# Two mixer layers on one core: normalised rows one step later in the first inverse stage, and another order for the last three rows before the second transform

## The chip, the core and the metric

The kernel runs on one core of a Trainium2 chip. Five engines work side by side, each through its own list in order: TensorE (PE in the profile, with its weight loads as PEld), VectorE (DVE), ScalarE (ACT), GpSimd (POOL) and SyncE (SP, which issues most of the transfers here). They wait for each other through semaphores. The metric is the time of one execution on the device, in microseconds (us); lower is better.

## The reference

Two kinds of layer alternate over an activation `x` of 2048 tokens by 640 channels, each kind twice and with the same weights both times:

```python
# A: global filter in the frequency domain
X = rfft2(x, axes=(-2, -1)) * (w_r + 1j * w_i)
y = irfft2(X, s=(S, D), axes=(-2, -1))

# B: token mixer, on the token axis, shared over channels
h = layernorm(x)                                   # over the channels
u = gelu(einsum("bsd,sf->bdf", h, w1) + b1)
y = einsum("bdf,fs->bds", u, w2) + b2              # then transposed back

x = x + A(layernorm(x)); x = x + B(layernorm(x))
x = x + A(layernorm(x)); x = x + B(layernorm(x))
```

S is 2048, D is 640, F is 1728, all in float32.

## The kernel before

The 2048 tokens lie as 16 rows of 128 partitions by 640 values (`NJ` = 16); one row of tokens is the unit of most loops. Products of 16-bit halves stand in for float32 ones: a value is kept as a high part and a low part (`fh`, `fl`; `hh`, `hl`; `wh`, `wl`), and three products (high by high, high by low, low by high) are summed in PSUM. A high part is written by ScalarE, the low part by VectorE as the difference. PSUM holds four tiles of two banks each (`big`), taken in turn.

`run` executes, twice: `a1` (transform along the tokens and channels, filter, first inverse), `a2` (last two inverse products, which give the new rows, and the layernorm in front of the mixer), and `b1st` or `b2nd` (the mixer). The first layer A's forward product `s1` is done at the start; the second one's is done inside `b1st`, row by row, as its rows become ready.

**`a2`, the inverse stage.** Its loop has one step a row, `i`, and works on several rows at a time. In step `i` TensorE makes `id_mm(i)`, 16 products, and `is1_mm(i-1)`, 6 products, whose operands are `eh` (ScalarE, from the result of `id_mm`) and `el` (VectorE, from the same result less `eh`). ScalarE copies part of the result of `is1_mm(i-2)` to `ec`, VectorE and then GpSimd add the result into the row `xt`, VectorE takes the row's statistics (`st`, `mv`, `v`, in the step after), GpSimd makes `r` and `nb` from them (one step later still), and ScalarE writes the normalised row `hf`, for rows 0 to 7 also its high part `hha`. Rows are loaded by SyncE into five buffers (`xload`), so a load waits until ScalarE has normalised the row five places earlier. `self.pin` holds the instructions of these loops in the order of the code. Behind the loop, `b1st` starts with the weights of the first two tiles of `w1`. Tile 13 of `w1` is the doubled one: 64 columns stand in it twice, and `wsplit` writes its high and low parts in halves, first ScalarE (`hi`), then VectorE (`lo`), one call for each of two chunks of eight rows of weights. Next `hl`, the low parts of the 16 normalised rows, is made on VectorE, and TensorE multiplies with them.

**The last rows of `b1st`.** Its second loop runs over the 16 rows of tokens, `j`. For each, TensorE sums the product with `w2` (82 products) into PSUM; ScalarE had added the bias to the old row, VectorE adds the product (`xt`), SyncE stores the row, and the row is prepared for the second layer A: statistics and `r`, `nb`, the normalised row `z` (`a0_norm`, ScalarE), sums and differences `eo` (`a0_fold1`, GpSimd) and `f` (`a0_fold2`, VectorE), `fh` (ScalarE), `fl` (VectorE). Then `s1` of the row: 15 small products on TensorE, `s1h` (ScalarE), `s1l` (VectorE). `pend` lists rows that are prepared and whose `s1` is still to come, and `flush(k)` issues them until `k` are left. The weights of the next row are split (`wsplit`) during the present row's product. Row 15 differs: its product is made for one half of the channels and then for the other, and `a0_tail` prepares it without waiting for the normalisation. In the kernel before, row 14's second half of the preparation stands in the middle of row 15's product, and its `fl` and `s1` stand inside `a0_tail`.

What follows, `a1`, starts with `dstage(0)`, whose products read `s1h` and `s1l` of all 16 rows.

All of these instructions go through the class `Pin`, so that the trace shows them under line 59; they are told apart by the names of the tiles.

Of the kernel before, what the change touches and what calls it, by code (L numbers as in the profile page):

```python
# [66 lines left out]
class Layers:  # L67
# [308 lines left out]
    def a0_tail(self, j, z, st, pend):  # L376

        V, G, T, p = self.V, self.G, self.T, self.pT
        mv = self.stats2(p, st)
        v = self.t(p, [128, 1], F32, "v", 2)  # L380
        V.tensor_scalar(v, mv[:, 1:2], self.CA, self.CB, op0=ALU.mult, op1=ALU.add)
        m2 = self.t(p, [128, 1], F32, "nm", 2)
        V.tensor_scalar(m2, mv[:, 0:1], 2.0, None, op0=ALU.mult)
        eo = self.t(p, [128, 646], F32, "eo", 2)
        v2 = lambda a, o, w: a[:, o:o + 2 * w].rearrange("p (a b) -> p a b", a=2)[:, :, 0:160]
        za, zb = v2(z, 1, 161), v2(z, 321, 160)
        G.tensor_tensor(v2(eo, 322, 161), za, zb, op=ALU.subtract)
        r = self.t(p, [128, 1], F32, "r", 2)
        G.tensor_tensor(r, v, self.mh, op=ALU.pow)
        V.scalar_tensor_tensor(v2(eo, 1, 161), za, m2, zb, op0=ALU.subtract, op1=ALU.add)  # L390
        V.tensor_scalar(eo[:, 0:162:161], z[:, 0:162:161], mv[:, 0:1], None, op0=ALU.subtract)
        sc = S1S / (ZS * TS)
        m = self.tM[j // 4]
        eb = eo[:, 0:644].rearrange("p (a b) -> p a b", a=2)
        ea, eb = eb[:, :, 0:160], eb[:, :, 161:321]
        fs = []
        for i, (c, w) in enumerate(((slice(0, 128), 512), (slice(128, 160), 128))):
            f = self.t(p, [128, w], F32, f"ft{i}", 1)
            f4 = f.rearrange("p (c b) -> p c b", c=4)
            V.tensor_tensor(f4[:, 0::3], ea[:, :, c], eb[:, :, c], op=ALU.add)  # L400
            V.tensor_tensor(f4[:, 1:3], ea[:, :, c], eb[:, :, c], op=ALU.subtract)
            if i:
                V.tensor_copy(f[:, 95:128:32], eo[:, 160:482:321])
            fh, fl = (self.t(p, [128, w], F16, f"{a}t{i}", 1) for a in ("fh", "fl"))
            T.activation(fh, f, AF.Identity, scale=r)
            fs.append((f, fh, fl))
        ps = []
        for k, f, fh in pend:
            ps.append((k, self.a0_s1(k, *self.a0_lo(f, fh))))
            self.a0_s1h(*ps[-1])  # L410
        qs = []
# [300 lines left out]
    def a2(self, li):  # L712
# [68 lines left out]
        for i in range(NJ + 5):  # L781
            has = [0 <= i - k < NJ for k in range(6)]
            if has[0]:
                pd[i] = id_mm(i)
            if has[1]:
                k = i - 1
                eh, ps = eo[k], pd.pop(k)
                el = elow(ps, eh)
                if not first and i == NJ:
                    self.pss0 = self.big()  # L790
                    for j in HA:
                        for a in range(2):
                            mm(self.pss0[:, a, :320], self.w[0][0][:, j], self.hh[j][:, a], start=j == 0, stop=False)
                p1[k] = is1_mm(eo.pop(k), el, tIM[k // 4][:, k % 4])
            if first and i == 10:
                next(sc)
            if has[4]:
                v, mean = vs.pop(i - 4)
                r = self.t(p, [128, 1], F32, "r", 2)
                G.tensor_tensor(r, v, self.mh, op=ALU.pow)  # L800
                b = self.t(p, [128, 1], F32, "nb", 2)
                G.tensor_scalar(b, mean, r, -1.0, op0=ALU.mult, op1=ALU.mult)
                rb[i - 4] = r, b
            if has[2]:
                k = i - 2
                x, ps = xt[k], p1.pop(k)
                o = ps[:, 1]
                e = self.t(p, [128, 324], F32, "ec", 2)
                T.activation(e[:, :322], ps[:, 0, :322], AF.Copy)
                V.tensor_tensor(v2(x, 160, NL), v2(x, 160, NL), v2(o, 161, 1), op=ALU.subtract)  # L810
                V.tensor_tensor(x[:, :NL], x[:, :NL], o[:, :NL], op=ALU.add)
                if first and i == 11:
                    next(sc)
                G.tensor_tensor(v2(x, 160, NL), v2(x, 160, NL), v2(e, 161, 1), op=ALU.add)
                G.tensor_tensor(x[:, :NL], x[:, :NL], e[:, :NL], op=ALU.add)
            if has[4]:
                r, b = rb.pop(i - 4)
                f = self.hf[i - 4]
                T.activation(f, xt.pop(i - 4)[:, :D].rearrange("p (a b) -> p a b", a=2), AF.Identity, scale=r, bias=b)
                if i - 4 in HA:  # L820
                    T.activation(self.hh[i - 4], f, AF.Copy)
            if 1 <= i and i + 1 < NJ:
                xt[i + 1] = xload(i + 1)
            if has[2]:
                nc.sync.dma_start(self.xs[li + 1][i - 2], xt[i - 2][:, :D])
            if has[3]:
                st = self.stats1(p, xt[i - 3])
                m = self.stats2(p, st)
                v = self.t(p, [128, 1], F32, "v", 2)
                V.tensor_scalar(v, m[:, 1:2], (1.0 + EPS) / ZS ** 2, EPS * EPS / ZS ** 2, op0=ALU.mult, op1=ALU.add)  # L830
                vs[i - 3] = v, m[:, 0:1]
            if has[0]:
                eo[i] = ehigh(pd[i])
            if i == 3:
                self.wload(1)
                self.wopen(1)
            if first:
                if i in (6, 7):
                    self.scan1(1, (i - 6,))
                if i == 8:  # L840
                    sc = self.scale1(1, at=lambda: p1[i - 1][:, 1, 400:401])
                    next(sc)
            if i in (12, 13):
                self.wsplit(1, (i - 12,), lo=False)
            if i in (1, 4, 8):
                mload()
        self.pin = False
# [81 lines left out]
    def b1st(self, li):  # L929
# [7 lines left out]
                T.activation(self.hh[j], self.hf[j], AF.Copy)  # L937
        sc = {m: self.scale1(m) for m in range(2, NFT + NJ)}
        self.pin = True
        self.wsplit(1, hi=False)  # L940
        self.wload(2)
        self.scan1(2)
        self.h = []
# [168 lines left out]
        def flush(k):  # L1112
            while len(pend) > k:
                self.s1_all(*pend.pop(0))

        for j in range(NJ):
            wh, wl = self.w.pop(NFT + j)
            ahead(NFT + j, (wh, wl))
# [3 lines left out]
            if j + 2 < NJ:  # L1122
                xts.append(load(j + 2))
            xt = xts[j][:, :D]
            T.activation(xt, xt, AF.Identity, bias=self.b2[:, j:j + 1])
            x2 = xt.rearrange("p (a b) -> p a b", a=2)
            tail = j == NJ - 1
            ps = self.big()
# [2 lines left out]
            if tail:  # L1131

                order.sort(key=lambda q: q[1])
                st = self.t(p, [128, 2, 6], F32, "st", 2)
                self.pin = True

            def half(a):
                V.scalar_tensor_tensor(x2[:, a], pss[a][:, :320], c2, x2[:, a], op0=ALU.mult, op1=ALU.add)
# [2 lines left out]
            for i, (ft, a) in enumerate(order):  # L1141
                if tail and i == NFT:
                    half(0)
                    flush(0)
                    pend.append((j - 1, *self.a0_hi(self.a0_fold2(late))))
                if i in (4, 8):
                    next(steps, None)
                if i in (6, 7):
# [11 lines left out]
            if tail:  # L1160
                half(1)
                nc.sync.dma_start(self.xs[li + 1][j], xt)
                self.a0_tail(j, xts[j], st, pend)
                self.pin = False
                break
            V.scalar_tensor_tensor(x2, ps[:, :, :320], c2, x2, op0=ALU.mult, op1=ALU.add)
            nc.sync.dma_start(self.xs[li + 1][j], xt)
            flush(1)
            r, b = self.stats_r(p, *self.stats(p, xt, self.CA, self.CB))
            late = self.a0_fold1(self.a0_norm(xt, r, b))  # L1170
            if j < NJ - 2:
                pend.append((j, *self.a0_lo(*self.a0_hi(self.a0_fold2(late)))))
        self.pop("a0")
        self.pop("u")
        self.pop("wr3")
# [798 lines left out]
```

## Time and profile before

| | |
|---|---|
| median of 3 runs | 1012.19 us (1011.85, 1012.19, 1015.22) |
| profiled execution | 1010.95 us |
| its span, first to last instruction | 1009.1 us |
| mean granted TensorE clock | 0.981 |
| VectorE busy | 781.1 us (77%) |
| ScalarE busy | 577.0 us (57%) |
| GpSimd busy | 297.9 us (30%) |
| first `a2` | 130 to 188 us |
| first `b1st`, from its first product to row 15's last | 183 to 556 us |
| second `a1` starts | 564.7 us |

TensorE is busy in most of the span, so a gain comes from stretches in which it stands still, or from fewer products. A row of the timeline gives the start in the span, the duration, the engine, the operation with what it writes and reads, and the partitions by elements. In brackets behind it stands the idle time of the engine ahead of it, with the operation that ended last before it went on. A row marked x4 stands for four instructions in a row, its duration for all of them together.

### The profile page before, as it was taken

How to read it: one execution, taken by the hardware profiler on the slowest of the kernel's cores; microseconds unless marked ns; L12 is line 12 of the kernel's file. 1: busy time of each engine (PE TensorE's matmuls, PEld its weight loads, DVE VectorE, ACT ScalarE, POOL GpSimd, SP SyncE). 2: the span in 40 equal slices, each digit the busy share in tenths (PEclk: the TensorE clock that was granted, in tenths of full speed). 3: DMA queues.
4: the chain of work that ended last, by engine and by line, in shares of the span. 5: the costliest groups of instructions: out<-in, count | busy, mean ns of one | idle time of the engine just before them, and what ended most of it. 6: DMA issues, size and time to landing. Idle time of an engine off the chain costs nothing.

```text
span 1009.1 us, 20992 instructions
## 1 busy us (share of the span) xinstructions
PE 966.7 (96%) x8235; PEld 720.8 (71%) x8235; DVE 781.1 (77%) x1493; ACT 577.0 (57%) x890; POOL 297.9 (30%) x502
## 2 busy tenths in 40 slices
PE   4889999999999999999999799999999999999998
PEld 3778777667777777777777687776777777677776
DVE  7978978988767885666666699789965567998885
ACT  5857668687666464555543376684734454444531
POOL 6937857512222202222222278574000000000000
PEclk9599999999999999999999999999999999999999
DMA  7865356657667636464431455465544346756411
GB/s 232 278 191 164 117 171 218 223 208 259 216 210 261 240 132 225 126 199 127 126 117 55 146 176 169 131 220 190 168 167 159 136 142 240 243 170 200 146 45 53
DMA packets 67258, 176.44 MB, mean 175 GB/s; under 512 B 7996, under 2 KB 15320, under 8 KB 67160
## 3 DMA queue, kind: packets, MB, share of 16 engines
q1 hardware_dynamic: 59384, 146.92, 45.0%
q0 software_dynamic: 7776, 28.20, 7.5%
q8 instruction: 64, 1.05, 0.4%
q14 instruction: 34, 0.28, 0.1%
HBM read 127.24 MB, written 47.84 MB: 174 GB/s over the span
## 4 chain that ended last, share of the span: by engine, by line
PE 48%; DVE 22%; ACT 12%; POOL 8%; issue 6%; DMA 4%; SPq 0%; ACTq 0%; DVEq 0%; POOLq 0%
PE ps L59 48%; DVE wl L59 3%; POOL eo L59 3%; DVE f L59 3%; DMA xt<-x 2%; DVE st L59 2%; DVE xt L59 2%; ACT junk L59 2%; ACT z L59 2%; ACT wh L59 2%; POOL xt L59 2%; DVE s1l L59 1%; DVE Yl L59 1%; ACT xt L59 1%; DVE hl L59 1%
## 5 line engine op out<-in xcount | busy, mean ns | idle before, releaser
L59 PEld LDWEIGHTS <-wh 128*128 128x128 f16 x2602 | 251.4, 98 | 101.3 <-issue 3.1
L59 PEld LDWEIGHTS <-wl 128*128 128x128 f16 x1610 | 157.5, 98 | 62.2 <-issue 1.0
L59 PE MATMUL ps<-ul,wh 128*128 128x320 f16 x448 | 133.1, 299 | 0.0
L59 PE MATMUL ps<-uh,wl 128*128 128x320 f16 x448 | 133.1, 299 | 0.0
L59 PE MATMUL ps<-uh,wh 128*128 128x320 f16 x416 | 124.3, 299 | 0.0
L59 PE MATMUL ps<-hl,wh 128*128 128x320 f16 x496 | 102.3, 299 | 0.9 <-DVE hl L59 0.9
L59 PEld LDWEIGHTS <-wo 128*128 128x128 f16 x756 | 73.9, 98 | 29.4 <-DVE wo L59 0.8
L59 DVE SCALAR_TENSOR_TENSOR wl<-raw,s,wh 128x896 f16<-128x896 f32 (+2 forms) x64 | 75.1, 1177 | 22.5 <-ACT wh L59 19.6
L59 POOL TENSOR_TENSOR r<-v,mh 128x1 f32<-128x1 f32 x64 | 36.3, 567 | 162.1 <-DVE nm L59 152.6
L59 ACT ACTIVATE junk<-raw 128x896 bf16<-128x896 f32 (+1 forms) x60 | 59.5, 992 | 27.6 <-DMA raw<-w 24.4
L59 PE MATMUL ps<-tDi,Yh 128*128 128x322 f16 x320 | 71.3, 300 | 0.2
L59 ACT ACTIVATE wh<-raw,s 128x896 f16<-128x896 f32 (+2 forms) x68 | 67.1, 1010 | 6.0 <-DVE s L59 5.5
L59 DVE TENSOR_TENSOR f<-eo 128x256 f32<-128x256 f32 (+1 forms) x124 | 39.0, 368 | 40.6 <-POOL eo L59 40.1
L59 POOL TENSOR_TENSOR xt<-xt,ec 128x320 f32<-128x320 f32 x64 | 52.4, 841 | 34.0 <-DVE xt L59 33.9
L59 ACT ACTIVATE z<-xt,nb,r 128x640 f32<-128x640 f32 x31 | 28.5, 919 | 57.0 <-POOL z L59 45.2
L59 PE MATMUL ps<-ph,tS 128*128 128x321 f16 (+2 forms) x288 | 58.5, 286 | 1.3 <-DVE tb L59 1.3
L59 PE MATMUL ps<-u,wo 128*128 128x320 f16 x420 | 59.0, 299 | 0.5 <-DVE wo L59 0.5
L59 DVE BATCH_NORM_STATS2 st<-xt 128x6 f32<-128x320 f32 x126 | 55.3, 481 | 5.2 <-DMA xt<-x 4.5
L59 PE MATMUL ps<-hha,wh 128*128 128x320 f16 x288 | 58.1, 299 | 0.9 <-DVE wh L59 0.9
L59 POOL TENSOR_TENSOR eo<-z 128x320 f32<-128x320 f32 x62 | 53.3, 880 | 17.1 <-ACT z L59 15.1
L59 PE MATMUL ps<-tM,f 128*128 128x128 f32 x160 | 39.5, 426 | 19.6 <-DVE f L59 19.6
L59 PE MATMUL ps<-tDi,Yl 128*128 128x322 f16 x192 | 55.7, 299 | 1.5 <-DVE Yl L59 1.5
(251 smaller groups left out, 2375.9 us busy)
## 6 DMA issues: line engine op xcount, KB each, us to landing
xt<-x SPq DMA_DIRECT2D x79, 320.0 KB
raw<-w SPq DMA_DIRECT2D x32, 512.0 KB
w<-w SPq DMA_DIRECT2D x48, 321.0 KB
x<-xt SPq DMA_DIRECT2D x47, 320.0 KB
raw<-w SPq DMA_DIRECT2D x32, 448.0 KB
raw<-w2z SPq DMA_DIRECT2D x32, 448.0 KB
w1S<-sp POOLq DMA_DIRECT2D x20, 512.0 KB, 3.7
out<-xt SPq DMA_DIRECT2D x15, 320.0 KB
```

The costliest lines, as they stand in the source:

```text
L59: i = f(*a, **k)
```

## The change

There are two parts that have nothing to do with each other but the kernel.

**In the first `a2`.** ScalarE's normalised row `hf` (with `hha`) is issued one step later, in step `i` for row `i-5` where it was `i-4`. Step 15 issues rows 10 and 11, and the rows after them stand where they stood. The load of a row moves with it: row `k` is loaded in step `k` where it was step `k-1`. `r` and `nb` get three buffers for two. The `lo` half of the doubled tile's first chunk moves from the start of `b1st` to the end of step 14. The second `a2` keeps its order.

**At the end of the first `b1st`.** From row 13 on the order is that of the code. Rows 13 and 14 are prepared by a generator `last` in four pieces, which the loop over the next row's products takes at positions 6, 12 and 17 of 28 (the first piece, the statistics, right behind the row). Half of `eo` is then made on VectorE. `s1` of rows 11 and 12 stands inside row 14's product; `s1` of rows 13 and 14 stands behind row 15's last product, ahead of row 15's own. The bias of row 15 is added together with row 14's.

```diff
@@ a0_tail
         V, G, T, p = self.V, self.G, self.T, self.pT
+        ps = [(k, self.a0_s1(k, *f)) for k, *f in pend]
+        for q in ps:
+            self.a0_s1h(*q)
         mv = self.stats2(p, st)
...
-        ps = []
-        for k, f, fh in pend:
-            ps.append((k, self.a0_s1(k, *self.a0_lo(f, fh))))
-            self.a0_s1h(*ps[-1])
         qs = []
@@ a2
-                r = self.t(p, [128, 1], F32, "r", 2)
+                r = self.t(p, [128, 1], F32, "r", 3)
...
-                b = self.t(p, [128, 1], F32, "nb", 2)
+                b = self.t(p, [128, 1], F32, "nb", 3)
...
-            if has[4]:
-                r, b = rb.pop(i - 4)
-                f = self.hf[i - 4]
...
-                if i - 4 in HA:
-                    T.activation(self.hh[i - 4], f, AF.Copy)
-            if 1 <= i and i + 1 < NJ:
-                xt[i + 1] = xload(i + 1)
+            for k in (i - 4,) if not first or i >= NJ else (i - 5,) if i < NJ - 1 else (i - 5, i - 4):
+                if not 0 <= k < NJ:
+                    continue
+                r, b = rb.pop(k)
+                f = self.hf[k]
...
+                if k in HA:
+                    T.activation(self.hh[k], f, AF.Copy)
+            k = i if first else i + 1
+            if 2 <= k < NJ:
+                xt[k] = xload(k)
...
+            if first and i == 14:
+                self.wsplit(1, (0,), hi=False)
@@ b1st
-        self.wsplit(1, hi=False)
+        self.wsplit(1, (1,), hi=False)
...
+        def last(j, xt):
+
+            rb = self.stats_r(p, *self.stats(p, xt, self.CA, self.CB))
+            yield
+            eo = self.a0_fold1(self.a0_norm(xt, *rb), sv=True)
+            yield
+            f = self.a0_hi(self.a0_fold2(eo))
+            yield
+            pend.append((j, *self.a0_lo(*f)))
+            yield
...
-            T.activation(xt, xt, AF.Identity, bias=self.b2[:, j:j + 1])
+            for k in {NJ - 2: (j, j + 1), NJ - 1: ()}.get(j, (j,)):
+                xk = xts[k][:, :D]
+                T.activation(xk, xk, AF.Identity, bias=self.b2[:, k:k + 1])
...
-                    flush(0)
-                    pend.append((j - 1, *self.a0_hi(self.a0_fold2(late))))
+                if j == NJ - 2 and i in (4, 20):
+                    flush(1)
+                if j >= NJ - 2 and i in (6, 12, 17):
+                    next(row)
...
+            self.pin = j >= NJ - 3
             V.scalar_tensor_tensor(x2, ps[:, :, :320], c2, x2, op0=ALU.mult, op1=ALU.add)
             nc.sync.dma_start(self.xs[li + 1][j], xt)
+            if self.pin:
+                row = last(j, xt)
+                next(row)
+                continue
             flush(1)
             r, b = self.stats_r(p, *self.stats(p, xt, self.CA, self.CB))
-            late = self.a0_fold1(self.a0_norm(xt, r, b))
-            if j < NJ - 2:
-                pend.append((j, *self.a0_lo(*self.a0_hi(self.a0_fold2(late)))))
+            pend.append((j, *self.a0_lo(*self.a0_hi(self.a0_fold2(self.a0_fold1(self.a0_norm(xt, r, b)))))))
```

Three places show how the instructions move. The first is ScalarE in the first `a2`, steps 3 to 5 (`eh` of a row, `ec` of the row two before, `hf` the normalised row, `hha` its high part; the numbers are those of tiles). Before:

```order
L59 ACTIVATE eh_2584<-ps_2543,cxe 128x644
L59 ACTIVATE ec_2622<-ps_2562 128x322
L59 ACTIVATE hf_367_2426<-xt_368_2445,nb_2620,r_2618 128x640
L59 ACTIVATE hha_867<-hf_367_2426 128x640
L59 ACTIVATE eh_2639<-ps_2592,cxe 128x644
L59 ACTIVATE ec_2673<-ps_2611 128x322
```

and in the change:

```order
L59 ACTIVATE eh_2583<-ps_2542,cxe 128x644
L59 ACTIVATE ec_2621<-ps_2561 128x322
L59 ACTIVATE eh_2636<-ps_2591,cxe 128x644
L59 ACTIVATE ec_2670<-ps_2610 128x322
L59 ACTIVATE hf_367_2426<-xt_368_2445,nb_2619,r_2617 128x640
L59 ACTIVATE hha_867<-hf_367_2426 128x640
L59 ACTIVATE eh_2687<-ps_2640,cxe 128x644
```

Row 0's `hf` and `hha` stood ahead of row 4's `eh`; now they stand behind it, ahead of row 5's.

The second place is VectorE in `b1st`, from the moment that row 13 (`xt_7143`) has its product, with the two chunks of `wl`, the weights of row 15. Before:

```order
L59 SCALAR_TENSOR_TENSOR xt_7143<-ps_7461,c_75,xt_7143 128x640
L59 SCALAR_TENSOR_TENSOR wl_7610<-raw_7137,s_73,wh_7609 128x896
L59 BN_STATS st_7577<-xt_7143 128x6 x2
L59 SCALAR_TENSOR_TENSOR s1l_5372<-ps_7559,s1h_5371 128x80x8
L59 BN_AGGR mv_7580<-st_7577 128x2
L59 SCALAR_TENSOR_TENSOR wl_7610<-raw_7139,s_73,wh_7609 128x896
L59 TENSOR_SCALAR v_7582<-mv_7580 128x1
L59 TENSOR_SCALAR nm_7584<-mv_7580 128x1
```

and in the change:

```order
L59 SCALAR_TENSOR_TENSOR xt_7143<-ps_7461,c_75,xt_7143 128x640
L59 BN_STATS st_7559<-xt_7143 128x6 x2
L59 BN_AGGR mv_7562<-st_7559 128x2
L59 TENSOR_SCALAR v_7564<-mv_7562 128x1
L59 TENSOR_SCALAR nm_7566<-mv_7562 128x1
L59 SCALAR_TENSOR_TENSOR s1l_5372<-ps_7589,s1h_5371 128x80x8
L59 SCALAR_TENSOR_TENSOR wl_7575<-raw_7137,s_73,wh_7574 128x896
L59 TENSOR_TENSOR eo_7618<-z_7615 128x2x160
L59 SCALAR_TENSOR_TENSOR wl_7575<-raw_7139,s_73,wh_7574 128x896
```

The row's `v` and `nm` now come ahead of both chunks of weights and of row 11's `s1l`, and a new `eo` stands between the two chunks.

The third place is VectorE's end of `a0_tail` (`ft`, `flt`: row 15's `f` and `fl` in two parts; `fl_7883`: row 14's). Before:

```order
L59 COPY ft_1096_7876<-eo_7864 128x2
L59 TENSOR_TENSOR fl_7883<-f_7806,fh_7812 128x640
L59 SCALAR_TENSOR_TENSOR flt_1095_7874<-ft_1093_7870,r_7866,fht_1094_7873 128x512
L59 SCALAR_TENSOR_TENSOR flt_1098_7881<-ft_1096_7876,r_7866,fht_1097_7880 128x128
L59 SCALAR_TENSOR_TENSOR s1l_5372<-ps_7885,s1h_5371 128x80x8
L59 SCALAR_TENSOR_TENSOR s1l_5372<-ps_7903,s1h_5371 128x64x8
L59 SCALAR_TENSOR_TENSOR s1l_5372<-ps_7917,s1h_5371 128x16x8
```

and in the change:

```order
L59 COPY ft_1098_7894<-eo_7882 128x2
L59 SCALAR_TENSOR_TENSOR flt_1097_7892<-ft_1095_7888,r_7884,fht_1096_7891 128x512
L59 SCALAR_TENSOR_TENSOR flt_1100_7899<-ft_1098_7894,r_7884,fht_1099_7898 128x128
L59 SCALAR_TENSOR_TENSOR s1l_5372<-ps_7842,s1h_5371 128x80x8
L59 SCALAR_TENSOR_TENSOR s1l_5372<-ps_7858,s1h_5371 128x80x8
L59 SCALAR_TENSOR_TENSOR s1l_5372<-ps_7902,s1h_5371 128x64x8
L59 SCALAR_TENSOR_TENSOR s1l_5372<-ps_7916,s1h_5371 128x16x8
```

Row 14's `fl` has left this place (it stands ahead of the second half of row 15's product sum), and row 13's `s1l` has come to it.

More of the change, by code (lines that the diff above doesn't have):

```diff
@@ L815, in a2 @@
                 G.tensor_tensor(x[:, :NL], x[:, :NL], e[:, :NL], op=ALU.add)
-            if has[4]:
-                r, b = rb.pop(i - 4)
-                f = self.hf[i - 4]
-                T.activation(f, xt.pop(i - 4)[:, :D].rearrange("p (a b) -> p a b", a=2), AF.Identity, scale=r, bias=b)
-                if i - 4 in HA:
-                    T.activation(self.hh[i - 4], f, AF.Copy)
-            if 1 <= i and i + 1 < NJ:
-                xt[i + 1] = xload(i + 1)
+            for k in (i - 4,) if not first or i >= NJ else (i - 5,) if i < NJ - 1 else (i - 5, i - 4):
[3 more added lines that the diff above has]
+                f = self.hf[k]
+                T.activation(f, xt.pop(k)[:, :D].rearrange("p (a b) -> p a b", a=2), AF.Identity, scale=r, bias=b)
+                if k in HA:
[3 more added lines that the diff above has]
+                xt[k] = xload(k)
             if has[2]:
@@ L1134, in b1st @@
                 st = self.t(p, [128, 2, 6], F32, "st", 2)
-                self.pin = True
             def half(a):
```

## The prediction

> **What bounds the kernel now.** I read the page's first part, then the windows by stage, then the timeline at every place where TensorE stands still.
>
> ```profile
> PE 966.7 (96%) x8235; PEld 720.8 (71%) x8235; DVE 781.1 (77%) x1493; ACT 577.0 (57%) x890; POOL 297.9 (30%) x502
> 380.00:520.00 140.00, 140.00 (x1139) 103.37 (x1137) 84.89 (x248) 74.86 (x109) 28.46 (x66) 1.00 0.49 157
> 561.10:564.20 3.10, 3.08 (x28) 2.90 (x28) 1.62 (x3) 0.90 (x2) 0.00 (x0) 0.54 0.37 106
> ```
>
> A windows row gives the stretch, its length, the busy time of PE, PEld, DVE, ACT and POOL, then the granted clock. TensorE is the bound: in 380 to 520 us it is busy 140.00 of 140.00. So time comes only from the 42.4 us (1009.1 - 966.7) in which it waits, and a wait removed early is kept if nothing behind it is bound by another engine. The change touches two such places. The larger is the end of the first `b1st`, behind row 15's last product at 555.9 us:
>
> ```profile
> 555.61 0.30 PE L59 MATMUL ps<-uh,wl 128*128 128x320 f16 x1
> 557.49 0.28 PE L59 MATMUL ps<-tM,fh 128*128 128x128 f16 x2 [1.59 <-ACT fh L59]
> 561.12 0.29 PE L59 MATMUL ps<-tM,fl 128*128 128x128 f16 x1 [3.34 <-DVE fl L59]
> 565.38 0.24 PE L59 MATMUL ps<-tD,s1l 128*128 128x160 f16 x1 [0.41 <-DVE s1l L59]
> 556.57 0.55 DVE L59 SCALAR_TENSOR_TENSOR zt<-ps,c,zt 128x320 f32<-128x320 f32 x1
> 559.10 1.03 DVE L59 TENSOR_TENSOR ft<-eo 128x256 f32<-128x256 f32 x4
> 560.24 0.82 DVE L59 TENSOR_TENSOR fl<-f,fh 128x640 f16<-128x640 f32 x1
> 560.98 1.00 DVE L59 SCALAR_TENSOR_TENSOR flt<-ft,r,fht 128x512 f16<-128x512 f32 x2
> 564.63 0.89 DVE L59 SCALAR_TENSOR_TENSOR s1l<-ps,s1h 128x512 f16<-128x512 f32 x2 [0.35 <-ACT s1h L59]
> 559.95 1.01 ACT L59 ACTIVATE fht<-ft,r 128x512 f16<-128x512 f32 x2 [2.52 <-DVE ft L59]
> ```
>
> TensorE waits 1.59 and 3.34 us there, then works for 3.1 us at a granted clock of 0.54 (the windows row). VectorE is the late one: row 14's `fl` stands in its list behind row 15's `ft` and ahead of its `flt`, and the first product of `dstage` that reads a low part starts only at 565.38. The second place is the first `a2` and the products behind it:
>
> ```profile
> 164.88 0.41 PE L59 MATMUL ps<-el,tIM 128*128 128x322 f32 x1 [0.51 <-DVE el L59]
> 171.51 0.41 PE L59 MATMUL ps<-el,tIM 128*128 128x322 f32 x1 [0.15 <-DVE el L59]
> 182.72 0.42 PE L59 MATMUL ps<-eh,tIM 128*128 128x322 f32 x1 [0.77 <-ACT eh L59]
> 202.91 3.28 PE L59 MATMUL ps<-hl,wh 128*128 128x320 f16 x23 [0.17 <-DVE hl L59]
>   DVE hl L59: 0.9, 4
> 161.52 0.92 ACT L59 ACTIVATE hf<-xt,nb,r 128x640 f32<-128x640 f32 x1 [1.21 <-POOL nb L59]
> 163.93 0.89 DVE L59 SCALAR_TENSOR_TENSOR el<-ps,cxe,eh 128x644 fp32r<-128x644 f32 x1 [1.00 <-ACT eh L59]
> 181.06 0.92 ACT L59 ACTIVATE hf<-xt,nb,r 128x640 f32<-128x640 f32 x1 [1.10 <-POOL nb L59]
> ```
>
> There TensorE waits 0.51 + 0.15 + 0.77 = 1.43 us, and 0.9 us more in four waits for `hl`. The cause is ScalarE's order: it stands 1.21 us at `hf` for GpSimd's `nb` while `eh` is queued behind it, so `el` comes 1.00 us late, and TensorE meets it.
>
> **The change part by part.** *Normalised rows one step later.* No instruction is added. When ScalarE comes to `hf`, its `nb` is a step old (3.3 us: 164.88 and 171.51 are two steps apart), so waits like the 1.21 us go. I take away 0.51 and 0.15 whole. At 182.72 the awaited `eh` of row 15 follows `hf` of row 11, which stays in step 15 and must still wait for its `nb` (the 1.10 us at 181.06). That moves only as far as the rows ahead of it do; I take 0.6 of the 0.77. Sum 1.3 us, bounds 0 and 1.43. It reaches the end only if VectorE's `hl` chain moves with it, since that chain ends the stretch (the waits up to 202.91).
>
> ```profile
> 189.62 1.40 DVE L59 SCALAR_TENSOR_TENSOR wh<-raw,s,wl 128x512 f16<-128x512 f32 x2
> 190.94 5.97 DVE L59 TENSOR_TENSOR hl<-hf,hha 128x640 f16<-128x640 f32 x8
> 185.78 0.89 DVE L59 TENSOR_TENSOR xt<-xt,ps 128x320 f32<-128x320 f32 x2
> 178.97 0.33 SPq L739 DMA_DIRECT2D xt<-x  x1
> 412.86 3.14 DMA xt<-x
> 375.88 9.19 DMA xt<-x
> ```
>
> *The doubled tile's split inside.* Of the two `wh` (1.40 us) ahead of `hl`, one, 0.70, moves to step 14. There VectorE has no gap, so `el` of rows 14 and 15 and all behind it come 0.70 later, and the start of `hl` gains 0.70 and loses 0.70: zero. Its cover is the wait at 182.72 and the `hha` products that are free to run there; without them it costs 0.70. It also lets SyncE issue a load of raw weights ahead of row 15's `xt`, with one issue of 0.33 us between. Row 15 was asked for at 178.97 and read by VectorE at 185.78, 6.8 us later. Now its load waits for row 10's `hf`, which stands just ahead of row 11's (181.06), so some 4.7 us are left against a load of 3.14. Cost zero, bound below under the rivals.
>
> *The last rows in pieces, two `s1` last.* I follow VectorE in the clock of before. Row 13's `xt` starts at 537.74 in both. Its `nm` no longer follows `wl` and `s1l`: row 14 took 2.74 from `xt` to `nm` with one `s1l` of 0.74 between, so 2.0 to 2.2 without. `nm` comes at 539.9 instead of 542.30, and `z` 1.02 behind it as before, 540.9 to 541.8.
>
> ```profile
> 537.74 0.88 DVE L59 SCALAR_TENSOR_TENSOR xt<-ps,c,xt 128x640 f32<-128x640 f32 x1
> 542.30 0.15 DVE L59 TENSOR_SCALAR nm<-mv 128x1 f32<-128x1 f32 x1
> 543.32 0.92 ACT L59 ACTIVATE z<-xt,nb,r 128x640 f32<-128x640 f32 x1 [3.90 <-POOL z L59]
> 544.32 1.69 POOL L59 TENSOR_TENSOR eo<-z 128x320 f32<-128x320 f32 x2 [1.00 <-ACT z L59]
> 541.23 1.10 DVE L59 SCALAR_TENSOR_TENSOR wl<-raw,s,wh 128x896 f16<-128x896 f32 x1
> 543.76 0.30 PE L59 MATMUL ps<-uh,wh 128*128 128x320 f16 x1
> 47.63 1.93 DVE L59 TENSOR_TENSOR f<-eo 128x256 f32<-128x256 f32 x4
> 512.38 1.03 DVE L59 TENSOR_TENSOR f<-eo 128x64 f32<-128x64 f32 x4 [2.71 <-POOL eo L59]
> 548.82 0.88 DVE L59 SCALAR_TENSOR_TENSOR xt<-ps,c,xt 128x640 f32<-128x640 f32 x1
> 551.56 0.14 DVE L59 TENSOR_SCALAR nm<-mv 128x1 f32<-128x1 f32 x1
> 549.33 0.28 PE L59 MATMUL ps<-tM,fh 128*128 128x128 f16 x2
> 550.17 0.30 PE L59 MATMUL ps<-uh,wh 128*128 128x320 f16 x1
> ```
>
> The new `eo` on VectorE is not in the trace. The bounds are 0.5 us (half of the 1.03 for the 640 elements of `ft`) and the 0.85 that GpSimd takes (1.69 for two). It reads the same `z` as GpSimd's half, and four `f` that overlap GpSimd's `eo` take 1.93 us where four alone take 1.03. So I let the two halves run one after the other: `eo` done at 542.4 on VectorE and 543.2 on GpSimd. The second `wl` of row 15 needs its `wh`, which ScalarE makes behind `z` in about 1 us, and runs from 542.8, or from 543.2 if it too is kept off by GpSimd, for 1.10 us. TensorE reads it at 544.3 (0.55 behind the first product at 543.76): met within 0.1 us, or with 0.4 to spare. Behind `wl` come `f`, `fl`, `s1l` and row 14's `xt`, which starts at 547.4 to 547.8 instead of 548.82. Once more the same steps, from `nm` to `z` to `eo` to `f`, bring row 14's `fl` to 555.6, or 556.4 with the halves apart.
>
> The Trainium skill ("SBUF — State Buffer", section "Who interferes with whom") says that a VectorE instruction with two SBUF inputs and a GpSimd one that reads SBUF lock each other out for a whole instruction, which speaks against splitting `eo` over the two. The trace agrees in kind (1.93 for 1.03); the later of the two figures is what that rule gives.
>
> Row 15's product ends at 555.07, not 555.9, because `s1` of row 13 (0.84 us, 549.33 to 550.17) has moved behind it. `zt` starts when `fl` is done, at 555.6 to 556.4 against 556.57. `ft` follows 2.53 later as before; `flt` no longer waits behind `fl`, only for `fht`, whose larger part is done some 1.5 behind `ft`'s start (0.85 to its own start, and by estimate 0.6 of its 1.01), so it starts at 559.6 to 560.45 against 560.98. Then the two `s1l` of rows 13 and 14 (0.74 apart, as `fl` and `flt` at 560.24 and 560.98 are) are the bound, since TensorE made those `s1` in its pause: 0.98 + 1.48 behind `flt`. Row 15's `s1l` starts at 562.1 to 562.9 against 564.63. Gain 1.7 to 2.5; I take 2.2, nearer the upper end, because ScalarE's end of `z` releases VectorE first in every such row. TensorE makes row 15's `s1` after 2.9 us of pause, so at the slow clock again; VectorE ends later all the same.
>
> Sum: 1.3 + 2.2 = 3.5 us, all of it on the path of TensorE, which is saturated behind both places. The profiled execution is 1010.95 us (span 1009.1 and 1.85 around it), so 1007.4; it lies 1.24 under the median of 1012.19, and the median goes to **1008.7 us**.
>
> **The rivals.** *Only the tail pays.* `hl` is VectorE's chain of 16 low parts, 11.9 us long, and nothing in it gets shorter. If step 14's 0.70 isn't covered, the chain starts no earlier and the 1.43 us turn into longer waits for `hl`. For it: the four waits there now. Against: `el` and all behind it hang on TensorE's pace, which moves. 1012.19 - 2.2 = 1010.0.
>
> *The tail pays half.* TensorE reaches row 15's second group before its `wl` (the margin above is 0.1 us), or its second half before row 14's `xt` has freed the PSUM tile that it takes over (its `xt` ends at 548.3 to 548.7; TensorE wants the tile at 549.3). A `z` that is 0.7 us late takes that from TensorE once and from the chain once: 2.2 - 1.4 leaves 0.8, with the first part 2.1, so 1010.1.
>
> *Slower: the loads of rows.* A row's load now has two steps, 6.6 us, where it had three, 9.9. The chain of waits holds one load of 9.19 us, at 375.88. Were the loads of this stage like it, a step would last half a load, 4.6 us instead of 3.3, and ten steps would lose 13 us: 1012.19 + 13 - 3.5 = 1021.7. It decides from 6.6 us a load. Against: the other loads in the chain take some 3.1, and no engine waits here for a row's load now.
>
> **How the numbers follow.** The forecast gets 0.68, the three rivals 0.15, 0.10 and 0.07. The forecast's own range is 2.7 to 4.3 us gained, 1007.9 to 1009.5. A measurement of this kernel can tell about 0.3%, 3.04 us, from no change; five sixths of the forecast's range lie beyond, 0.57. Within: 0.11 of the forecast and the first two rivals, 0.36. Slower: 0.07. The range goes down to the forecast's own lower end less 0.7 for the spread of the runs (two of the three lie 0.34 apart), and up to both parts at their least (0 and 0.8, 1011.4): 1007.2 to 1011.6.
>
> **What would show it.** In the first `a2`, `hf` without a wait for `nb` up to step 14, and TensorE without a wait for `el`; the first `hl` product run ends 1.3 us earlier. At the tail, row 13's `s1` behind row 15's last product, `flt` directly behind `ft`, and less than 8 us, against 9.8, from row 15's last product to the first low part in `dstage`. It is wrong if VectorE's `eo` takes over 0.85, if TensorE waits for `wl` in row 15, or if `xt` waits for its load.

## The result, and the profile after

The changed kernel takes 1008.24 us (median of 13 runs, 1007.10 to 1010.51) against 1012.01 for the kernel before in 13 runs beside it: a ratio of 0.9959, 95% interval 0.9948 to 0.9971, so 3 to 5 us less. The profiled execution is 1007.18 us with a span of 1005.4, against 1010.95 and 1009.1. The prediction said 1008.7 and 3.5 us. That is met, but two of its terms were too small and one that it had set at nothing was 1.6 us, so the trace is worth reading place by place.

First the page's first part and TensorE's timeline in the first `a2` of the changed kernel. The first number is the start, the second the modelled duration, the bracket the idle time ahead of it and what ended it:

```profile
PE 968.0 (96%) x8235; PEld 722.8 (72%) x8235; DVE 781.9 (78%) x1495; ACT 577.9 (57%) x890; POOL 298.9 (30%) x500
...
160.62 0.42 PE L59 MATMUL ps<-eh,tIM 128*128 128x322 f32 x1
160.88 0.31 PE L59 MATMUL ps<-el,tIM 128*128 128x322 f32 x1
...
163.72 0.42 PE L59 MATMUL ps<-eh,tIM 128*128 128x322 f32 x1
163.98 0.31 PE L59 MATMUL ps<-el,tIM 128*128 128x322 f32 x1
...
180.99 0.41 PE L59 MATMUL ps<-eh,tIM 128*128 128x322 f32 x1 [0.58 <-ACT eh L59]
...
200.64 4.64 PE L59 MATMUL ps<-hl,wh 128*128 128x320 f16 x33 [0.17 <-DVE hl L59]
```

The waits for `el` are gone, the one for `eh` is 0.58 instead of 0.77, and the last wait for `hl` stands at 200.64 instead of 202.91. ScalarE's rows, two of them:

```profile
177.78 0.91 ACT L59 ACTIVATE hf<-xt,nb,r 128x640 f32<-128x640 f32 x1
179.34 0.92 ACT L59 ACTIVATE hf<-xt,nb,r 128x640 f32<-128x640 f32 x1 [0.65 <-POOL nb L59]
```

`hf` doesn't wait for `nb` up to step 14; the one wait is row 11's in step 15. Then the tail, TensorE first, VectorE behind it:

```profile
552.62 0.30 PE L59 MATMUL ps<-uh,wl 128*128 128x320 f16 x1
552.76 0.28 PE L59 MATMUL ps<-tM,fh 128*128 128x128 f16 x2
557.13 0.40 PE L59 MATMUL ps<-tM,fht 128*128 128x128 f16 x2 [2.53 <-ACT fht L59]
559.85 0.45 PE L59 MATMUL ps<-tD,s1h 128*128 128x160 f16 x2 [0.37 <-ACT s1h L59]
560.58 0.32 PE L59 MATMUL ps<-tD,s1l 128*128 128x160 f16 x1 [0.28 <-DVE s1l L59]
534.58 0.88 DVE L59 SCALAR_TENSOR_TENSOR xt<-ps,c,xt 128x640 f32<-128x640 f32 x1
552.24 0.81 DVE L59 TENSOR_TENSOR fl<-f,fh 128x640 f16<-128x640 f32 x1
552.96 0.55 DVE L59 SCALAR_TENSOR_TENSOR zt<-ps,c,zt 128x320 f32<-128x320 f32 x1
557.11 1.01 DVE L59 SCALAR_TENSOR_TENSOR flt<-ft,r,fht 128x512 f16<-128x512 f32 x2 [0.38 <-ACT fht L59]
558.04 1.55 DVE L59 SCALAR_TENSOR_TENSOR s1l<-ps,s1h 128x640 f16<-128x640 f32 x2
```

Row 13's `s1` stands behind row 15's last product, row 14's `fl` ahead of `zt`, and `flt` waits for `fht` alone. From row 15's last product to the first low part in `dstage` it is 7.96 us (552.62 to 560.58), before 9.77 (555.61 to 565.38). But the windows of the changed kernel, cut at the edges where its granted clock changes (the columns are those of the prediction's rows), show what was not foreseen:

```profile
553.68:557.09 3.41, 0.92 (x17) 0.74 (x14) 2.77 (x11) 2.15 (x4) 1.33 (x2) 1.00 0.25 96
557.09:560.51 3.42, 2.41 (x17) 1.57 (x17) 3.16 (x6) 1.04 (x3) 0.00 (x0) 0.50 0.36 96
560.51:563.92 3.41, 3.34 (x26) 3.35 (x27) 0.21 (x2) 0.11 (x1) 0.00 (x0) 0.50 0.93 322
563.92:567.33 3.41, 3.41 (x37) 2.85 (x36) 1.90 (x4) 1.48 (x3) 0.00 (x0) 1.00 0.60 176
```

TensorE has `dstage` to do from 560.58, and does it at half clock until 563.92. The kernel before stood better, in the same view:

```profile
553.74:557.15 3.41, 2.16 (x16) 1.33 (x14) 2.48 (x7) 0.80 (x2) 1.66 (x3) 1.00 0.00 0
557.15:560.56 3.41, 0.28 (x2) 0.11 (x2) 3.13 (x12) 0.89 (x2) 1.41 (x2) 1.00 0.25 96
560.56:563.98 3.42, 2.87 (x28) 2.87 (x28) 1.95 (x4) 1.11 (x3) 0.00 (x0) 0.50 0.34 96
```

There the half clock ended at 563.98, ahead of `dstage`'s first product (564.65).

**Where the time came from.** I take the same matmul in two kernels and subtract its starts, at six places of TensorE: an `eh` product ahead of the change (154.89 in before), one behind the `hl` chain (209.70), one of a late row of `b1st` (520.06), the first low part (565.38), one in `dstage` (589.99), one in the second `a2` (639.95). The differences of neighbouring shifts are what a stretch gained or lost:

| stretch | before | changed kernel | gain |
|---|---|---|---|
| up to 154.89 | 154.89 | 154.98 | -0.09 |
| first `a2` and `hl` | 209.70 | 207.43 | **2.36** |
| to the tail | 520.06 | 517.91 | -0.12 |
| tail, to the first low part | 565.38 | 560.58 | **2.65** |
| `dstage`'s start | 589.99 | 586.76 | **-1.57** |
| to the second `a2` | 639.95 | 636.19 | 0.53 |

The sum is 3.76. The last line isn't the change's: the twelve kernels below, those with the old tail among them, all have it, 0.31 to 0.56, against this one execution of before, so that execution lost it.

### The profile page after: what moved, and what is told of

The parts are those of the page before. It is cut to its first block, busy times and chain, and to the rows that moved or that the text cites. A ratio compares the mean times of both kernels' runs of the same rounds, so it can differ in the third digit from the quotient of the medians.

```text
span 1005.4 us, 21003 instructions
## 1 busy us (share of the span) xinstructions
PE 968.0 (96%) x8235; PEld 722.8 (72%) x8235; DVE 781.9 (78%) x1495; ACT 577.9 (57%) x890; POOL 298.9 (30%) x500
## 4 chain that ended last, share of the span: by engine, by line
PE 51%; DVE 24%; ACT 9%; POOL 6%; issue 5%; DMA 5%; SPq 0%; ACTq 0%; POOLq 0%; DVEq 0%
PE ps L59 51%; DVE wl L59 3%; DVE f L59 3%; DVE st L59 3%; DMA xt<-x 3%; POOL eo L59 3%; DVE s1l L59 2%; DVE xt L59 2%; DVE Yl L59 2%; ACT wh L59 2%; ACT junk L59 1%; ACT z L59 1%; DVE hl L59 1%; POOL xt L59 1%; DVE ta L59 1%
```

## The experiments

Twelve kernels, in the order of the questions. The four columns on the right are gains by the same matmuls, each from one profiled execution against the one of before; "both" is the sum of the two columns ahead of it. Ratios are of times, each to runs of before taken beside it, with 95% intervals.

| kernel | ratio to before | median us | first `a2` | to first low part | `dstage`'s start | both |
|---|---|---|---|---|---|---|
| changed | 0.9959 (0.9948 to 0.9971) | 1008.24 | 2.36 | 2.65 | -1.57 | 1.08 |
| after_again | 0.9969 (0.9958 to 0.9979) | 1007.50 | 2.37 | 2.66 | -1.77 | 0.89 |
| a_only | 0.9979 (0.9968 to 0.9991) | 1009.36 | 2.36 | 0.17 | -2.12 | -1.95 |
| b_only | 0.9991 (0.9978 to 1.0003) | 1010.86 | -0.02 | 2.66 | -1.72 | 0.94 |
| no_split | 0.9959 (0.9943 to 0.9975) | 1006.90 | 2.26 | 2.66 | -1.70 | 0.96 |
| eo_gp | 0.9969 (0.9957 to 0.9982) | 1008.72 | 2.35 | 1.81 | -2.43 | -0.62 |
| s13_early | 0.9968 (0.9957 to 0.9979) | 1008.43 | 2.37 | 1.82 | -1.46 | 0.36 |
| before_fill | 0.9980 (0.9970 to 0.9990) | 1010.03 | -0.01 | 1.15 | -0.14 | 1.01 |
| a_fill | 0.9957 (0.9942 to 0.9972) | 1006.82 | 2.36 | 1.17 | -0.36 | 0.81 |
| fill | 0.9955 (0.9939 to 0.9971) | 1006.27 | 2.35 | 3.00 | -1.12 | 1.88 |
| fill_first | 0.9963 (0.9950 to 0.9976) | 1007.14 | 2.36 | 3.00 | -1.55 | 1.45 |
| fill_swap | 0.9962 (0.9949 to 0.9976) | 1007.09 | 2.38 | 1.61 | 0.01 | 1.62 |
| fill_swap2 | 0.9959 (0.9945 to 0.9973) | 1006.28 | 2.36 | 2.80 | 0.01 | 2.81 |

The times can't tell most of these from one another (an interval is 2 to 3 us wide). The local gains can. That of the first `a2` repeats within 0.03 us in the ten kernels that have this part whole. In the four with the whole new tail and no added matmuls (changed, after_again, b_only, no_split), the gain up to the first low part repeats within 0.01 and that at `dstage`'s start within 0.2.

**The two parts by themselves.** a_only has the hunks of `a2` and the one line at `b1st`'s start; b_only all the others.

> The kernel before with the a2 part alone (normalised rows and row loads one step later, three buffers, half of the wh split in step 14); the tail is that of before. Theory 1, TensorE's losses counted from start to start of its matmuls, as the changed kernel's trace gives them: the first hl run of products ends 2.2 to 2.5 us earlier than in before, and the end comes 2.2 to 2.5 earlier too, give or take one slow window of the clock at the tail (up to 1.7 us). Ratio 0.9975 to 0.9980. Theory 2, the prediction's sum of the waits in the idle column: 1.3 us, ratio 0.9987. Rival (only the tail pays): 0, ratio 1.000.

> The kernel before with the b1st part alone (rows 13 and 14 in pieces, half of eo on VectorE, two s1 last); the first a2 is that of before. Theory 1: from row 15's last product to the first product that reads a low part 8.0 us instead of 9.8, that product 2.4 to 2.7 earlier than in before; behind it the half clock gives back 0 to 1.7 us, by where the clock's windows of 3.41 us fall, so 1.0 to 2.7 us at the end. Ratio 0.9973 to 0.9990. Theory 2, the prediction: all of 2.2 us reaches the end, ratio 0.9978. Rival (the tail pays half): 0.8 us, with a wait of TensorE in row 15's product.

In a_only the first `a2` gained 2.36, theory 1 and not my sum; all of it reached the tail, less 0.27. There the earlier tail met the clock's windows otherwise:

```profile
553.32:556.73 3.41, 0.28 (x2) 0.11 (x2) 3.10 (x12) 0.74 (x1) 1.41 (x2) 1.00 0.25 96
556.73:560.15 3.42, 1.96 (x19) 1.97 (x20) 2.29 (x7) 1.37 (x3) 0.00 (x0) 0.50 0.29 96
560.15:563.56 3.41, 2.76 (x23) 2.18 (x21) 1.71 (x3) 1.11 (x3) 0.00 (x0) 0.50 0.27 107
563.56:566.97 3.41, 3.41 (x28) 3.41 (x26) 0.50 (x1) 0.73 (x2) 0.00 (x0) 0.50 0.93 315
```

Three slow windows in a row, and 1.95 us lost. In b_only the tail gained 2.66 to the first low part and lost 1.72 behind it. So in these traces the parts don't add: the tail's part is worth 0.94 to before's tail and 3.03 (1.08 + 1.95) once `a2` has moved it. By the ratios a_only is 2.1 us faster (0.9 to 3.2), b_only 0.9 (from 2.2 faster to 0.3 slower), both at once 4.1 (2.9 to 5.3): there 2.1 + 0.9 against 4.1 lies within the intervals, and a_only gains more than the 0.41 (2.36 - 1.95) that its trace nets. How much of the 1.95 comes back in every execution is open.

**The split moved to step 14.** no_split undoes one edit of `a2`:

```diff
-            if first and i == 14:
-                self.wsplit(1, (0,), hi=False)
...
-        self.wsplit(1, (1,), hi=False)
+        self.wsplit(1, hi=False)
```

> The changed kernel with both low halves of the doubled tile's first chunk made at the start of b1st again. Theory 1, the prediction: that move is worth zero, so the first hl run ends within 0.2 us of the changed kernel's, and the ratio is the changed kernel's (0.996). Rival 1: the move is what gave the part of the gain that no wait in the idle column explains (0.30 and 0.22 us behind step 15), so hl ends 0.5 to 0.7 later than in the changed kernel. Rival 2: the move costs, and hl ends 0.2 to 0.7 earlier without it.

2.26 instead of 2.36: worth 0.1, the prediction's zero. Rival 1 falls, though the 0.30 and 0.22 behind step 15 did hang on it: without the move the whole comes at row 15's `eh` instead.

**VectorE's half of `eo`.** eo_gp has `sv=False` in `last`.

> The changed kernel with both halves of eo of rows 13 and 14 on GpSimd. Theory 1: VectorE has slack in both rows now (row 14's fl ends 0.7 us ahead of row 15's second half), so the loss of 0.5 to 0.7 us a row is met by it: first low part within 0.4 us of the changed kernel's, ratio 0.996. Theory 2: the half on VectorE shortens each row's chain by 0.85, two rows in a row, and the first low part comes 0.8 to 1.4 us later, ratio 0.997. Rival (lock): the two halves run one after the other anyway, so nothing changes at all, below 0.1 us.

The first low part comes 0.84 later (1.81 for 2.65), theory 2 at its lower end. Row 14's `fl` is then late for `s1` (`fl` and `fht` in TensorE's timeline), and `fht` waits 0.58 longer:

```profile
554.52 0.23 PE L59 MATMUL ps<-tM,fl 128*128 128x128 f16 x1 [0.43 <-DVE fl L59]
558.54 0.29 PE L59 MATMUL ps<-tM,fht 128*128 128x128 f16 x2 [3.11 <-ACT fht L59]
```

In the changed kernel the two halves overlap in part. VectorE's and GpSimd's rows, the last one GpSimd's half of row 15 by itself:

```profile
538.77 0.49 DVE L59 TENSOR_TENSOR eo<-z 128x320 f32<-128x320 f32 x1
538.81 1.18 POOL L59 TENSOR_TENSOR eo<-z 128x320 f32<-128x320 f32 x1 [1.07 <-ACT z L59]
...
553.60 0.86 POOL L59 TENSOR_TENSOR eo<-zt 128x320 f32<-128x320 f32 x1 [3.52 <-DVE zt L59]
```

GpSimd's half takes 1.18 beside VectorE's and 0.86 alone, so 0.32 of VectorE's 0.49 comes back as a longer half on GpSimd. The two together take 1.22 (538.77 to 539.99), where 0.49 + 0.86 one after the other would be 1.35 and both on GpSimd took 1.69. The rival falls with the 0.84.

**Row 13's `s1` behind row 15.** s13_early puts it back to the middle of row 15's product:

```diff
                 if tail and i == NFT:
                     half(0)
+                    flush(0)
```

> The changed kernel with s1 of row 13 in the middle of row 15's product, where before had it, and row 14's alone behind it. Theory 1: row 15's product ends 0.84 us later, and so do zt, ft, flt and the first low part, as TensorE's product is what VectorE's last rows wait for: ratio 0.9968. Theory 2: VectorE's own chain is the bound there, and nothing is lost, ratio 0.996. Rival: less idle time in the window of the clock ahead of dstage, so its half clock ends a window (3.41 us) sooner, and the end comes 0.7 earlier all the same.

0.83 lost at the first low part, theory 1 to 0.01; the rival falls (1.46 given back, 0.1 less than in the changed kernel).

**The clock.** In `a0_tail`, `fill` adds matmuls whose result nobody reads, into the second bank of a tile whose first bank takes row 15's `s1` (`fh` of row 14 as the moving operand): 15 ahead of `fht`'s products, 8 behind `flt`'s.

```diff
+    def idle(self, qt, w, x, n):
+        for _ in range(n):
+            self.PE.matmul(qt[:, 1, :320], w, x[:, :320], start=True, stop=True)
...
-            q = self.big()[:, 0, :n]
+            qt = self.big()
+            q = qt[:, 0, :n]
+            if not i:
+                self.idle(qt, m[:, j % 4, 0], pend[-1][1], 15)
...
+            if i:
+                self.idle(qt, m[:, j % 4, 0], pend[-1][1], 8)
```

> The changed kernel with 15 matmuls of 128x320 that nobody reads in TensorE's first pause behind row 15's product and 8 in its second (ahead of dstage), into a half of a PSUM tile that nothing uses. Clock theory: the granted clock stays 1.00 from 552 to 566 us, the products behind the first low part follow each other at 0.07 us instead of 0.13, dstage's first ph on ScalarE comes 1.3 to 1.7 us earlier than in the changed kernel, and so does the end: ratio to before 0.994 to 0.995. Rival 1: these products wait for something else (their operands, the PSUM), so the clock is 1.00 and the time that of the changed kernel, ratio 0.996. Rival 2: the added matmuls end too late, fht's product starts behind them, and up to 1 us is lost.

The clock was 1.00 throughout (TensorE's rows and two windows of this kernel):

```profile
552.50:556.00 3.50, 3.13 (x35) 2.30 (x32) 2.91 (x12) 2.07 (x4) 1.42 (x2) 1.00 0.24 94
556.00:559.40 3.40, 2.59 (x28) 1.91 (x28) 3.24 (x6) 1.23 (x4) 0.00 (x0) 1.00 0.32 97
...
559.31 0.30 PE L59 MATMUL ps<-tD,s1h 128*128 128x160 f16 x2
559.58 0.24 PE L59 MATMUL ps<-tD,s1l 128*128 128x160 f16 x1
...
567.16 0.23 PE L59 MATMUL ps<-tD,stk 96*128 96x160 f16 x1 [0.82 <-DMA stk<-rest]
```

The first low part comes 0.35 earlier, and `dstage`'s products follow at 0.07 us, so the clock theory's mechanism is shown. Of the 1.92 us that it should give (0.35 + 1.57), 0.80 is left: a wait that the half clock had covered, for `stk`, appears.

before_fill and a_fill put such matmuls into the old tail, 10 ahead of row 14's `s1` and 21 between its second product and its third.

> The kernel before with 10 matmuls of 128x320 that nobody reads ahead of row 14's s1 (its pause of 1.59 us) and 21 between that s1's first two products and its third (its pause of 3.34 us). Clock theory: the granted clock stays 1.00 from 550 to 570 us; the first product with a low part, set by VectorE, comes within 0.3 us of before's, and dstage runs at 0.07 us a product, as it did in before's profiled execution, where the half clock ended 1.4 us ahead of it. So little in that execution (0 to 0.4), and over the runs as much as the half clock reaches dstage in others of them: 0 to 1 us, ratio 0.999 to 1.000. Rival: the half clock is a cost in before too (1.6 us as in the changed kernel), ratio 0.9984.

> The a2 part alone with the same 31 matmuls in the tail. Clock theory: a2 alone lost 1.9 us at the tail to three slow windows (556.7 to 567.0 us); with the clock held at 1.00 the tail gives back what a2 gained, no more and no less, so from row 15's product to dstage as in before, 2.3 us earlier at the end than the kernel before with the same matmuls. Ratio to before 0.9965 to 0.9977. Against the changed kernel with its fillers it lacks the tail's part: 2.7 us at the first low part, 1.7 at the end, since there the load of stk took 1.0. Rival: a2's gain is lost at the tail to something else, and the ratio is 0.9985 or more.

Here I was wrong on before_fill: the half clock costs before too, as its rival said, 1.15 us ahead of the first low part (`s1` of rows 14 and 15 ran at half clock there) and 0.9980 in the times. a_fill gains at the tail 0.81 where a_only lost 1.95; the rest of `a2`'s gain is untouched, so it was the clock that took it. With the clock held, the tail's part is worth 1.83 at the first low part (3.00 - 1.17) and 1.07 behind it (1.88 - 0.81). It also means that 31 idle matmuls in the old tail do nearly what the new tail does: a_fill gains 3.17 by the matmuls (2.36 + 0.81) and the changed kernel 3.44 (2.36 + 1.08), and their ratios are 0.9957 and 0.9959.

fill_first leaves out the 8 of the second pause:

> The changed kernel with the 15 matmuls of the first pause alone; the second pause, ahead of dstage, stays empty. Clock theory (a window of 3.41 us in which TensorE has less than about 0.6 of work makes the next one slow): the window at 553.7 to 557.1 is filled, so s1 of row 15 runs at 1.00; the next, 557.1 to 560.5, holds about 1.5 us of work, so the window from 560.5 to 563.9 is slow again and dstage's first products with it. The first low part 0.2 to 0.4 earlier than in the changed kernel, the end 0 to 0.6 earlier: ratio 0.9955 to 0.996. Rival: only a pause of 2.5 us in one piece brings the half clock, so with the first one filled the clock is 1.00 up to 566 us, as with all 23.

```profile
553.57:556.99 3.42, 3.33 (x39) 2.50 (x36) 3.11 (x12) 1.79 (x3) 1.42 (x2) 1.00 0.25 96
556.99:560.40 3.41, 1.50 (x17) 0.95 (x17) 3.03 (x6) 1.40 (x4) 0.00 (x0) 1.00 0.31 96
560.40:563.82 3.42, 3.32 (x25) 3.33 (x26) 0.24 (x2) 0.09 (x1) 0.00 (x0) 0.50 0.96 349
```

The window with 1.50 of 3.41 us of work has no pause over 0.6 us, and the next one is slow: the rival falls, and at this tail it is the little work in a window that goes with the half clock, not one long pause. 0.35 is gained at the first low part, as expected.

**The wait for `stk`.** `stk` is read back from a copy in memory of the pieces of 128 of `s1h` and `s1l`. fill_swap evicts those first: `for pv, q in qs[::-1]:`.

> The changed kernel with all 23 matmuls, and the last two evictions of row 15's s1 in the other order: the piece of 128 first, that of 512 behind it. With the clock held, dstage waits 0.82 us for stk, which is read back from a copy of the pieces of 128 and so hangs on their s1l. Theory: that copy is issued 0.7 us earlier, the wait for stk falls to 0.2 or less, the first low part comes 0 to 0.3 later, and the end 0.5 to 0.8 earlier than with the matmuls alone: ratio 0.9945 to 0.995. Rival: the load of stk itself, not its store, is late, and nothing is gained or 0.3 lost.

It lost 1.39 at the first low part: my 8 matmuls stood in the tile of the small piece, so its eviction waited for them. fill_swap2 gives them a tile of their own.

> The two evictions of row 15's s1 swapped as in the run before, but the 8 matmuls of the second pause now go to a PSUM tile of their own: in the run before they stood in the tile of the piece of 128, so its eviction waited for them and the first low part came 1.4 us later. Theory: with that removed, the store of the small pieces is issued some 0.7 us earlier than with the 23 matmuls alone, the wait for stk (0.82 us there) falls to 0.2 or less, the first low part comes within 0.3 us of that kernel's, and from row 15's product to dstage's end 0.4 to 0.8 us more is gained: ratio 0.9945 to 0.9955. Rival: the load of stk is late whatever its store does (two hops through memory one after the other), and the time is that of the 23 matmuls alone.

SyncE's issues and TensorE's first use of `stk` in fill_swap2:

```profile
560.60 0.32 SPq L494 DMA_DIRECT2D rest<-s1l  x1
562.61 2.38 SPq L488 DMA_DIRECT2D stk<-rest  x3
...
568.02 0.23 PE L59 MATMUL ps<-tD,stk 96*128 96x160 f16 x1
```

No wait is left, and the tail gains 2.81, 0.93 more than with `fill` and 1.73 more than the changed kernel. It is the best version by the local gains. By the times it isn't shown: 1006.28 (6 runs), 0.9959 (0.9945 to 0.9973), beside the changed kernel's 0.9959 and 0.9969; its own profiled execution began 1.37 us late.

after_again is the changed kernel once more.

> The changed kernel once more, beside the two others, for a second profile of it. If the windows of the clock stand at the same place of the program in every execution, the tail loses 1.5 to 1.7 us to the half clock here too and nets 1.0 to 1.1 at dstage, with the first a2 at 2.35 and the first low part at 2.66 as before; if they stand anywhere, what the half clock takes differs by up to 1.7. Ratio 0.996.

Each of the four columns repeats, within 0.2 us where `dstage`'s start is in it and within 0.01 in the other two.

## Why the prediction was right, and where it was not

*The first `a2`: 1.3 predicted, 2.36 measured, outside its upper bound of 1.43.* The mechanism was right, the size was read wrongly, in the step "TensorE waits 0.51 + 0.15 + 0.77". The idle column begins at the modelled end of the matmul ahead. Undisturbed, the next matmul starts before that end: in the changed kernel `el` at 163.98 starts 0.26 behind an `eh` of 0.42. A wait as long as this overlap doesn't show at all, and a longer one shows shortened by it. In the kernel before:

```profile
160.53 0.42 PE L59 MATMUL ps<-eh,tIM 128*128 128x322 f32 x1
160.96 0.41 PE L59 MATMUL ps<-el,tIM 128*128 128x322 f32 x1
...
163.95 0.41 PE L59 MATMUL ps<-eh,tIM 128*128 128x322 f32 x1
164.88 0.41 PE L59 MATMUL ps<-el,tIM 128*128 128x322 f32 x1 [0.51 <-DVE el L59]
165.13 0.46 PE L59 MATMUL ps<-eh,tIM 128*128 128x322 f32 x2
```

From `eh` to `el` it is 0.93 (163.95 to 164.88) where the undisturbed pair of the changed kernel has 0.26, and the `el` product itself holds up the next by 0.25 instead of 0.15. The column's 0.51 costs 0.77, and the whole step moved by 0.81. At 160.53 the pair is 0.17 longer and the column shows no wait at all; that step gained 0.28. The column's two waits for `el`, 0.66, were worth 1.6 with the hidden ones (0.28, 0.81 and 0.39 at the `el` of 160.96, 164.88 and 171.51, and 0.14 at an `eh` at 178.10); what is left, 0.2 at row 15's `eh` and 0.5 between there and the last `hl`, is near the 0.6 that I had taken. The `hl` chain did move with TensorE, so "only the tail pays" falls.

*The split: zero; measured 0.1. The row loads: nothing.* No engine waits for one there, and the slower rival falls.

*The tail to the first low part: 2.2 (1.7 to 2.5) predicted, 2.65 measured.* The 0.84 of row 13's `s1` is right (s13_early), `eo` on VectorE takes 0.49, at its lower bound of 0.5, TensorE meets no late `wl` (it is busy 17.60 of the 17.60 us from 535 to 552.6), so "the tail pays half" falls. The step that failed is "row 13's `xt` starts at 537.74 in both". It starts at 534.58, which in before's clock (2.15 earlier at 520.06) is 536.73, 1.0 earlier; and `zt` behind row 14's `fl`, 552.96, is 555.1 there, 0.5 to 1.3 earlier than I had it. The likely reason is an edit that I didn't price: row 15's bias moves to the end. In before ScalarE does it beside the first rows, and VectorE meets a late `wl` behind it:

```profile
393.78 0.81 ACT L59 ACTIVATE zt<-zt,b2s 128x640 f32<-128x640 f32 x1
407.05 1.15 DVE L59 SCALAR_TENSOR_TENSOR wl<-raw,s,wh 128x896 f16<-128x896 f32 x1 [0.97 <-ACT wh L59]
```

In the changed kernel that `wl` is not waited for, and VectorE is nearer to TensorE by about 1.0 us from there on. From the last product of a row to the row's `xt` it is 6.42 us at row 2, ahead of this `wl`, and 6.63 at row 3 in before, but 6.31 and then 5.59 in the changed kernel. At row 13 it is 6.92 in before, 5.91 in the changed kernel, 0.8 to 1.5 less than before in all ten kernels of the table with the new tail, and 0 to 0.2 less in the three with the old one. That the bias is the cause, and that this lead makes up the rest of the 2.65 (0.84 + 0.84 + 1.0), is argued from these rows; no run moved the bias alone, and none tested the pieces' order by itself.

*The half clock: nothing predicted, 1.57 measured.* "so at the slow clock again; VectorE ends later all the same" holds for row 15's `s1`, and stops there. I took the half clock as belonging to the pause; it belongs to windows of 3.41 us, and the second slow one reached 3.3 us into `dstage`, which is TensorE's own. The Trainium skill ("TensorE: Matmul & The Clock Gate", section "Part 1: The HAM clock gate") has that window, free-running. By its rule that half clock follows an idle window neither 557.09 nor fill_first's 560.40 would have been slow: 0.92 and 1.50 us of work stood ahead of them, and the trace decides.

So 1.06 and 0.45 too little, 1.57 too much: the forecast was met because its errors cancelled, which is luck, not because each step was right. One figure of the chances was also off: of the range from 2.7 to 4.3 us four fifths, not five sixths, lie beyond 3.04, which makes 0.54 of the 0.57.

## What to carry to other kernels

Price a wait of TensorE from start to start, against the same pair undisturbed, and not by the idle column: here 0.66 us in the column was 1.6. Ahead of every pause that a change shortens or moves, lay out the clock's windows and ask which work falls into the next slow one; work in the pause that nobody reads can be worth about as much as the shortened pause (by the matmuls 1.01 in before_fill, 0.94 in b_only). And when a scheduler sets the order, price moved instructions at the place that they leave as well as the one where they go.

## What the runs showed of the hardware

At this tail full clock became half behind windows in which TensorE had 0.28, 0.92, 0.97 (eo_gp) and 1.50 us of work, and stayed behind 1.8 (eo_gp) and more. From half it came back behind 2.87 and more, not behind 2.41, 2.52 or 2.76. An idle window isn't needed for it, nor a long pause. These figures are no rule for other stages: in the float32 products at the start of the same traces full clock fell behind 1.91 (before, 51.98) and 2.04 us (eo_gp, 17.30), and half clock stayed behind 3.03 and 3.04 (before, 38.33 to 45.16).

The windows also stand at almost the same place of the program. All edges of one profile lie on one grid of 3.41 us, so the grid can be counted on to the tail in all fourteen profiles. The edge nearest to 553.7 us, less the shift of the `eh` product at 154.89, lies between 553.45 and 554.04, 0.6 us of the 3.41 that it could take. It is not so from the start. Taken the same way at the matmul that before has at 43.17 us, the place in the grid is spread over 2.5 us; at 63.43 us, near the end of the first run of `dstage`'s products, over 0.6, while the starts themselves have spread from 0.9 to 3.0 us. Most of that run lies between the two, at 0.07 us a product at full clock (before, 60.8 to 63.4) and at 0.13 at half clock (before_fill, 61.7 to 64.6). So the executions fall into step with the windows there, and the loss at the tail repeats as far as these profiles show. That the half clock in that run does it is a guess; no run tried it.
